# A SwiGLU block on Trainium2: a second way to split u for the three-product form, five shared PSUM banks, split weights for ten channel blocks

## The chip, the cores and the metric

One core of a Trainium2 chip runs the whole kernel. The metric is the device time of one execution in microseconds (us): the median of 3 runs, 1662.22 us before the change (1661.70 to 1662.46). The profile is one execution of the same program, with a span of 1660.3 us. The engines are TensorE (PE; its weight loads are a row of their own, PEld), VectorE (DVE), ScalarE (ACT), GpSimd (POOL) and SyncE (SP), which issues the transfers.

## The reference

An attention block with 32 inducing points feeds a feed-forward block (SwiGLU without bias). 49,664 rows of 128 channels go through both.

```python
# attention: B, N, m, C = 4, 12416, 32, 128
h = mab(I, x)            # softmax(scale * I @ x^T) @ x, over all N rows of a batch
attn_out = mab(x, h)     # softmax(scale * x @ h^T) @ h

# feed-forward: d_model 128, d_ff 1536
rms = np.sqrt(np.mean(x * x, axis=-1, keepdims=True) + 1e-06)
xn = x / rms * rms_g
g = xn @ w_gate
silu = g * (1.0 / (1.0 + np.exp(-g)))
val = xn @ w_val
return (silu * val @ w_out).astype(np.float32)
```

`u = silu * val` is the operand that the change is about: it is multiplied with `w_out` (called `wo` below) in float32 accuracy.

## The kernel before

**Units and slots.** A batch is cut into 25 units: 20 of 512 columns, 4 of 480 and 1 of 256, so there are 100 units. The 1536 channels of the feed-forward block are 12 blocks of 128 (j = 0 to 11). One unit and one block are a slot: 1200 slots. A slot has a gate matmul into one PSUM bank, silu on ScalarE, the output products that are due, a value matmul into a second bank, and the product u on VectorE.

```python
def slot(j, products, steps, tanh):
    g = ps_gv.tile([P, 512], F32, name="gv", tag="gv")
    nc.tensor.matmul(g[:, 0:T], sg[:, ts(j, P)], a[:, 0:T], start=True, stop=True)        # L657
    ...
        nc.scalar.activation(sl[:, 0:T], g[:, 0:T], AF.Silu)                              # L665
    products()
    v = ps_gv.tile([P, 512], F32, name="gv", tag="gv")
    nc.tensor.matmul(v[:, 0:T], sv[:, ts(j, P)], a[:, 0:T], start=True, stop=True)        # L668
    t = up.tile([P, 512], F32, name="u")
    ...
        nc.vector.tensor_tensor(out=t[:, 0:T], in0=sl[:, 0:T], in1=v[:, 0:T], op=ALU.mult) # L674
    steps()
    if (b, u, j) in ready:
        soon(1, lambda: three(j, t))
    else:
        plain.append(lambda: project(wo[:, j, :], t[:, 0:T]))
```

**Two forms of the output product.** In the plain form, `wo[:, j, :]` times u is one float32 matmul; the profile has it as two MATMUL and two LDWEIGHTS records. In the three-product form, u and wo are each split into a high and a low half in the type fp32r, and three fp32r matmuls take the place of the float32 one: high by high and low by low into a bank of their own (`u3`), and the product of differences into `acc`.

```python
def three(j, t):
    ...                                                     # one of 4 places in each of the rings hi, lo, d
    nc.scalar.activation(hi, v, AF.Copy, scale=1.0 - 2.0 ** -13)                          # L644
    nc.gpsimd.tensor_tensor(out=lo, in0=v, in1=hi.bitcast(F32), op=ALU.subtract)          # L645
    def rest():
        hs = third.tile([P, 512], F32, name="hs")
        nc.scalar.activation(hs[:, 0:T], hi.bitcast(F32), AF.Copy, scale=1.0 + 2.0 ** -12) # L649
        nc.gpsimd.tensor_tensor(out=d, in0=hs[:, 0:T], in1=v, op=ALU.subtract)            # L650
        kara.append((ready[b, u, j], lambda: project3(j, hi, lo, d)))
    soon(1, rest)

def project3(j, hi, lo, d):
    ...
    nc.tensor.matmul(ups[:, 0:T], w[:, i, :], hi, ...)      # L622
    nc.tensor.matmul(ups[:, 0:T], w[:, NK + i, :], lo, ...) # L624
    if not st["k"]:
        o = st["o"] = outp.tile([P, 512], F32, name="o")
        nc.scalar.activation(o[:, 0:T], ups[:, 0:T], AF.Copy, scale=1.0 + 2.0 ** -12)     # L627
    project(w[:, 2 * NK + i, :], d)                         # L606, as is the plain form
```

`soon(1, f)` runs f among the steps of the next slot. Engines take their instructions in the order in which the program has them. `finish` adds `u3` and `acc` (L614) and turns the result (L615), both on VectorE.

**Which slots take the three-product form.** The split weights exist for five blocks (`KJ` is 0, 2, 5, 7 and 9). A ledger of one server, with a slot of 1.25 us and 2.75 us for each split, chooses among these; it also gives the slot from which the three matmuls may be issued.

```python
SLOT, SPLIT, RESERVE = 1.25, 2.75, 3
...
    free = max(free, now) + busy.get(k, 0) + seam_busy.get((b, u, j), 0)
    begin = max(free, now + 2.2 * SLOT)
    if (j not in KJ or b == 0 and u < 2 or (b, u) == flat[-1] or begin > now + 3.2 * SLOT or
            any(k - 2 <= e <= k + 6 for e in marks)):
        continue
    free = begin + SPLIT
    ready[b, u, j] = int((free + 0.3) / SLOT) + 1
```

**When products are issued.** Each slot issues one product, or two if more than `RESERVE` are waiting; a three-product that has reached its slot goes first, and a plain one is kept back by at least one slot.

**PSUM.** Eight banks: four for gates and values (`ps_gv`), two for `acc`, one for `u3`, one (`ps_m`) for the attention of the next batch and the seams (the rms factors and attention weights of the next units).

Of the kernel before, what the change touches and what calls it, by code (L numbers as in the profile page):

```python
# [24 lines left out]
def kernel(  # L25
# [74 lines left out]
    KJ = [j for j in range(NJ - 2) if j % 5 in (0, 2)] + [NJ - 3]  # L100
    NK = len(KJ)
    SLOT, SPLIT, RESERVE = 1.25, 2.75, 3
# [10 lines left out]
    wp = pool("wp", NC)  # L113
# [8 lines left out]
    ps_gv = pool("ps_gv", 4, space=PSUM)  # L122
    ps_acc = pool("ps_acc", 2, space=PSUM)
    ps_u = pool("ps_u", 1, space=PSUM)
    ps_m = pool("ps_m", 1, space=PSUM)
# [30 lines left out]
    gam = const.tile([P, 1], F32, name="gam")  # L156
    nc.scalar.dma_start(out=gam[:], in_=moe_rms_g.rearrange("(c o) -> c o", o=1))
# [6 lines left out]
    bias = const.tile([P, 1], F32, name="bias")  # L164
    nc.vector.memset(bias[:], -896.0 * (1 << 23))
    ones = const.tile([P, 1], F32, name="ones")
    nc.vector.memset(ones[:], 1.0)
# [10 lines left out]
    sel = const.tile([P, 2, R, m], F32R, name="sel")  # L178
    nc.gpsimd.memset(sel[:].bitcast(F32), 0.0)
# [10 lines left out]
    ps = ps_m.tile([P, 512], F32, name="mm", tag="mm")  # L190
# [27 lines left out]
    def rounding(i, c):  # L218
# [10 lines left out]
        def numbers(name, add, mul, engine):  # L229

            t, to = st[name], st[name] if name == "e" else st[name].bitcast(F32)
            if engine is nc.scalar and name == "e":
                nc.scalar.activation(to[:], t[:], AF.Relu, bias=bias[:], scale=mul)
            elif engine is nc.scalar:
                nc.scalar.activation(to[:], t[:], AF.Copy, bias=add, scale=mul)
            else:
                engine.tensor_scalar(out=to[:], in0=t[:], scalar1=mul, scalar2=add, op0=ALU.mult, op1=ALU.add)

        def power():
            if i < 2:  # L240
                t = w0[i, c] = (silp.tile([P, 512], F32, name="silu") if (i, c) == (1, 0) else
                                 third.tile([P, 512], F32, name="hs") if (i, c) == (1, 1) else
                                 wp.tile([P, 512], F32, name="w"))
                dst = st["dst"] = t[:]
            else:
                dst = st["dst"] = wo.rearrange("p j c -> p (j c)")[:, ts(c, 512)]
            if not wide:
                nc.sync.dma_start(out=dst if i < 2 else dst.rearrange("p (j c) -> p j c", c=C), in_=source(i, c))
                return
            words = raw[i, c].rearrange("p (f w) -> p f w", w=2)  # L250
            st["low"], st["high"] = words[:, :, 0], words[:, :, 1]
            e = st["e"] = work.tile([P, 512], I32, name="we", tag="work")
            nc.vector.tensor_scalar(out=e[:], in0=st["high"], scalar1=20, scalar2=0x7FF,
                                    op0=ALU.logical_shift_right, op1=ALU.bitwise_and)
# [35 lines left out]
    lent = []  # L290

    def attention(b, load_next):
# [8 lines left out]

        def bank():
            if flowing:
                assert not lent
                return ps_m.tile([P, 512], F32, name="mm", tag="mm")
            return ps_gv.tile([P, 512], F32, name="gv", tag="gv")
# [42 lines left out]
        def max3():  # L349
            ps = bank()  # L350
            nc.tensor.matmul(ps[:, 0:1], st["row4"][:].rearrange("p q m -> p (q m)"), ones[0:1, 0:1],
                             start=True, stop=True)
            nbias = st["nbias"] = small.tile([P, 1], F32, name="nbias")
            nc.vector.tensor_copy(out=nbias[:], in_=ps[:, 0:1])
# [57 lines left out]
        def scale_h():  # L412
            hg = st["hg"] = once.tile([P, P], F32, name="hg")
            nc.vector.tensor_scalar_mul(out=hg[:], in0=st["hT"][:], scalar1=gam[:])
# [35 lines left out]
        def fetch(i):  # L450
            st["w", i] = [wp.tile([P, 512], F32, name="w") for c in range(NC)]
            for w, d in zip(st["w", i], w32[i]):
                nc.sync.dma_start(out=w[:], in_=d[:])

        def stack(i):
# [3 lines left out]
            for c, w in enumerate(st.pop(("w", i))):  # L459
                nc.tensor.matmul(ps[ts(c, m), :], st["hg"][:, 0:m], w[:], start=True, stop=True)  # L460
# [10 lines left out]
        def stack_of(i, c):  # L471

            ps = st["stack", i, c] = bank()
            nc.tensor.matmul(ps[:], st["hg"][:], w0.pop((i, c))[:], start=True, stop=True)  # L474
            nc.scalar.copy(out=stacks[b][i][:, ts(c, 512)], in_=ps[:])
# [14 lines left out]
    def seam(b, s):  # L490
# [13 lines left out]
        def square():  # L504
            assert not lent
            lent.append(s)
            ps = st["ps"] = ps_m.tile([P, 512], F32, name="mm", tag="mm")
            nc.tensor.matmul(ps[rows, 0:w], gram[b][rows, rows], st["eT"][rows, 0:w], start=True, stop=True)  # L508

        def turn_z():  # L510
            ps = st["ps"]
            lent.clear()
# [41 lines left out]
    def spread(b, u):  # L554
# [5 lines left out]
        ps = ps_gv.tile([P, 512], F32, name="gv", tag="gv")  # L560
# [7 lines left out]
    kws = {}  # L568
# [5 lines left out]
    def split_wo(step):  # L574

        if not step:
            kws["w"] = xnp.tile([P, 3 * NK, C], F32R, name=f"xn{full - 1}")
        w = kws["w"]
        whi, wlo, ws = (w[:, ts(k, NK), :] for k in range(3))
        if step == 0:  # L580
            for i, j in enumerate(KJ):
                nc.vector.tensor_scalar_mul(out=whi[:, i, :], in0=wo[:, j, :], scalar1=1.0 - 2.0 ** -13)
        if step == 1:
            for i, j in enumerate(KJ):
                nc.vector.tensor_tensor(out=wlo[:, i, :], in0=wo[:, j, :], in1=whi[:, i, :].bitcast(F32), op=ALU.subtract)
        if step == 2:
            nc.vector.tensor_scalar_mul(out=wlo, in0=wlo.bitcast(F32), scalar1=4096.0)
        if step == 3:
            nc.vector.tensor_tensor(out=ws, in0=wlo.bitcast(F32), in1=whi.bitcast(F32), op=ALU.subtract)
            for k, name in enumerate(("hi", "lo", "d")):  # L590
                kws[name] = xnp.tile([P, 4, 512], F32R, name=f"xn{full - 4 + k}")

    def ffn(b, u):
# [17 lines left out]
        def finish():  # L611
# [3 lines left out]
            nc.vector.transpose(out=o[:, 0:T], in_=(o if nk else acc)[:, 0:T])  # L615
            soon(2, lambda: store(o))

        def project3(j, hi, lo, d):
            if st["k"] == nk:
                st["u"] = ps_u.tile([P, 512], F32, name="u3")  # L620
            ups, i, w = st["u"], KJ.index(j), kws["w"]
            nc.tensor.matmul(ups[:, 0:T], w[:, i, :], hi, start=st["k"] == nk, stop=False)  # L622
            st["k"] -= 1
            nc.tensor.matmul(ups[:, 0:T], w[:, NK + i, :], lo, start=False, stop=not st["k"])  # L624
# [3 lines left out]
            project(w[:, 2 * NK + i, :], d)  # L628
# [10 lines left out]
        def three(j, t):  # L639

            n = kws["n"] = (kws.get("n", 0) + 1) % 4
            hi, lo, d = (kws[name][:, n, 0:T] for name in ("hi", "lo", "d"))
            v = t[:, 0:T]
            nc.scalar.activation(hi, v, AF.Copy, scale=1.0 - 2.0 ** -13)  # L644
            nc.gpsimd.tensor_tensor(out=lo, in0=v, in1=hi.bitcast(F32), op=ALU.subtract)  # L645

            def rest():
                hs = third.tile([P, 512], F32, name="hs")
                nc.scalar.activation(hs[:, 0:T], hi.bitcast(F32), AF.Copy, scale=1.0 + 2.0 ** -12)  # L649
                nc.gpsimd.tensor_tensor(out=d, in0=hs[:, 0:T], in1=v, op=ALU.subtract)  # L650
                kara.append((ready[b, u, j], lambda: project3(j, hi, lo, d)))

            soon(1, rest)

        def slot(j, products, steps, tanh):
            g = ps_gv.tile([P, 512], F32, name="gv", tag="gv")
# [10 lines left out]
            v = ps_gv.tile([P, 512], F32, name="gv", tag="gv")  # L667
            nc.tensor.matmul(v[:, 0:T], sv[:, ts(j, P)], a[:, 0:T], start=True, stop=True)  # L668
            t = up.tile([P, 512], F32, name="u")
# [85 lines left out]
    nc.scalar.activation(tiny[:], ones[:], AF.Silu)  # L755
# [25 lines left out]

    def schedule(b):


        plan, marks, busy = {}, [], {}

        def add(k, step, *args):
            plan.setdefault(int(k), []).append(lambda: step(*args))
            if getattr(step, "__name__", "") == "sub_max" and args[0]:
                busy[int(k)] = 1.1  # L790

        def exponentials(k, step, first):

            groups = list(range(first, NS - 1, 2))
            for i, s in enumerate(groups):
                add(k + i, step, s, NS if s == groups[-1] else s + 2)
                if i:
                    by_tanh.add((b, k + i))
            return k

        if not b:
# [8 lines left out]
            for step in range(4):  # L810
                add(18 + 2 * step, split_wo, step)
# [34 lines left out]
        return plan, marks, busy  # L846


    seams, seam_busy = {}, {}
    order = [(b, s) for b in range(B) for s in range(NS)]  # L850
    firsts = {s: min(u for u, one in enumerate(units) if one[0] == s) for s in range(NS)}
    for k, (b, s) in enumerate(order):
# [5 lines left out]
        for late_by, one in enumerate(following):  # L858
            for i, step in enumerate(seam(*one)):
# [4 lines left out]
                seam_busy[at] = seam_busy.get(at, 0) + {3: 3.0, 4: 1.2, 6: 1.4}.get(i, 0)  # L864
# [7 lines left out]
    free, ready = 0.0, {}  # L872
    for b, u in flat:
        plan, marks, busy = plans[b]
        for j in range(NJ):
            k = u * NJ + j
            now = (b * NU * NJ + k) * SLOT
            free = max(free, now) + busy.get(k, 0) + seam_busy.get((b, u, j), 0)
            begin = max(free, now + 2.2 * SLOT)
            if (j not in KJ or b == 0 and u < 2 or (b, u) == flat[-1] or begin > now + 3.2 * SLOT or  # L880
                    any(k - 2 <= e <= k + 6 for e in marks)):
                continue
            free = begin + SPLIT
            ready[b, u, j] = int((free + 0.3) / SLOT) + 1

    for b in range(B):
        plan, marks, _ = plans[b]
# [74 lines left out]
```

## Time and profile before

| | |
|---|---|
| time, median of 3 runs | 1662.22 us |
| span of the profiled execution | 1660.3 us |
| busy: PE, PEld | 1647.4 us (99%), 1037.4 us (62%) |
| busy: DVE, ACT, POOL | 1173.5, 1235.9, 1159.4 us (71, 74, 70%) |
| slots in the three-product form | 400 of 1200 (L645: 400 records) |
| granted TensorE clock | 1.000 of full speed |

The busy time of PE is the union of its records, whose ends are modelled and which overlap; how closely matmuls follow one another is read from the starts in the timeline. A group of instructions (line, engine, operation, out<-in, shape) comes with its busy time, the mean duration of one in ns, and the idle time of its engine just ahead of it with what ended it.

### The profile page before, as it was taken

How to read it: one execution, taken by the hardware profiler on the slowest of the kernel's cores; microseconds unless marked ns; L12 is line 12 of the kernel's file. 1: busy time of each engine (PE TensorE's matmuls, PEld its weight loads, DVE VectorE, ACT ScalarE, POOL GpSimd, SP SyncE). 2: the span in 40 equal slices, each digit the busy share in tenths (PEclk: the TensorE clock that was granted, in tenths of full speed). 3: DMA queues.
4: the chain of work that ended last, by engine and by line, in shares of the span. 5: the costliest groups of instructions: out<-in, count | busy, mean ns of one | idle time of the engine just before them, and what ended most of it. 6: DMA issues, size and time to landing. Idle time of an engine off the chain costs nothing.

```text
span 1660.3 us, 23265 instructions
## 1 busy us (share of the span) xinstructions
PE 1647.4 (99%) x6780; PEld 1037.4 (62%) x6780; DVE 1173.5 (71%) x1949; ACT 1235.9 (74%) x2234; POOL 1159.4 (70%) x931
## 2 busy tenths in 40 slices
PE   8999999999999999999999999999999999999998
PEld 6546566655666665665666656665567666666666
DVE  4887776676767877667677787667766666666665
ACT  4567777767787787776778777777687788788786
POOL 1347766767577775776578777577657888888885
PEclk9999999999999999999999999999999999999999
DMA  6455524333353141633335313252211111111111
GB/s 256 89 80 92 91 48 95 89 89 66 60 91 60 35 87 32 132 77 79 60 66 81 59 36 85 62 119 74 47 31 37 34 33 39 32 33 39 32 38 25
DMA packets 389167, 112.39 MB, mean 68 GB/s; under 512 B 365072, under 2 KB 369712, under 8 KB 386480
## 3 DMA queue, kind: packets, MB, share of 16 engines
q1 hardware_dynamic: 388304, 110.82, 33.0%
q8 instruction: 54, 0.88, 0.2%
q14 instruction: 73, 0.60, 0.1%
q10 hardware_dynamic: 736, 0.08, 0.0%
HBM read 53.95 MB, written 27.00 MB: 49 GB/s over the span
## 4 chain that ended last, share of the span: by engine, by line
PE 97%; DVE 2%; ACT 0%; POOL 0%; issue 0%; DVEq 0%; POOLq 0%
PE acc L606 45%; PE gv L657 17%; PE gv L668 16%; PE u L624 5%; PE u L622 5%; PE mm L330 3%; PE mm L508 1%; PE mm L386 1%; PE gv L321 0%; PE acc L187 0%; DVE u L674 0%; PE gv L330 0%; PE mm L460 0%; PE mm L474 0%; POOL rs L523 0%
## 5 line engine op out<-in xcount | busy, mean ns | idle before, releaser
L674 DVE TENSOR_TENSOR u<-silu,gv 128x512 f32<-128x512 f32 (+2 forms) x1186 | 779.8, 664 | 433.8 <-PE gv L668 228.5
L665 ACT ACTIVATE silu<-gv 128x512 f32<-128x512 f32 (+2 forms) x1186 | 691.4, 584 | 352.6 <-PE gv L657 310.0
L606 PE MATMUL acc<-u,wo 128*128 128x512 f32 (+2 forms) x1600 | 791.4, 579 | 1.2 <-DVE u L674 1.2
L668 PE MATMUL gv<-a,sv 128*128 128x512 f32 (+2 forms) x1188 | 757.7, 638 | 0.9 <-DVE u L674 0.9
L645 POOL TENSOR_TENSOR xn<-u,xn 128x512 fp32r<-128x512 f32 (+2 forms) x400 | 504.2, 1260 | 356.1 <-ACT xn L644 312.5
L650 POOL TENSOR_TENSOR xn<-hs,u 128x512 fp32r<-128x512 f32 (+2 forms) x400 | 503.9, 1260 | 32.6 <-ACT hs L649 27.8
L657 PE MATMUL gv<-a,sg 128*128 128x512 f32 (+2 forms) x1188 | 482.6, 406 | 0.0
L657 PEld LDWEIGHTS gv<-a,sg 128*128 128x128 f32 x1188 | 224.1, 189 | 228.0 <-ACT silu L665 110.8
L606 PEld LDWEIGHTS acc<-u,wo 128*128 128x128 f32 x1600 | 298.5, 188 | 79.3 <-issue 16.0
L668 PEld LDWEIGHTS gv<-a,sv 128*128 128x128 f32 x1188 | 224.0, 189 | 194.4 <-issue 133.8
L644 ACT ACTIVATE xn<-u 128x512 fp32r<-128x512 f32 (+2 forms) x400 | 247.7, 619 | 25.6 <-DVE u L674 23.4
L649 ACT ACTIVATE hs<-xn 128x512 f32<-128x512 f32 (+2 forms) x400 | 245.9, 615 | 5.6 <-POOL xn L650 4.7
L606 PE MATMUL acc<-xn,xn 128*128 128x512 f32 (+2 forms) x400 | 156.6, 391 | 0.0
L624 PE MATMUL u<-xn,xn 128*128 128x512 f32 (+2 forms) x400 | 155.6, 389 | 0.0
L622 PE MATMUL u<-xn,xn 128*128 128x512 f32 (+2 forms) x400 | 155.2, 388 | 0.0
L523 POOL TENSOR_TENSOR rs<-ms,mhalf 128x16 f32<-128x16 f32 (+2 forms) x28 | 75.9, 2711 | 16.1 <-DVE ms L521 14.0
L606 PEld LDWEIGHTS acc<-xn,xn 128*128 128x128 f32 x400 | 74.9, 187 | 19.4 <-POOL xn L650 2.8
L624 PEld LDWEIGHTS u<-xn,xn 128*128 128x128 f32 x400 | 75.1, 188 | 18.4
L622 PEld LDWEIGHTS u<-xn,xn 128*128 128x128 f32 x400 | 75.0, 188 | 16.9 <-issue 0.7
L615 DVE STREAM_TRANSPOSE o<-o 128x512 f32<-128x512 f32 (+2 forms) x97 | 67.7, 698 | 3.4
L614 DVE TENSOR_TENSOR o<-acc,o 128x512 f32<-128x512 f32 (+2 forms) x97 | 64.9, 669 | 0.1
L627 ACT ACTIVATE o<-u 128x512 f32<-128x512 f32 (+2 forms) x97 | 56.4, 581 | 0.0
(169 smaller groups left out, 769.6 us busy)
## 6 DMA issues: line engine op xcount, KB each, us to landing
out_dram<-o SPq DMA_DIRECT2D x320, 64.0 KB, 1.9
xT<-in_x_dram SPq DMA_DIRECT2D x60, 256.0 KB, 5.3
xn<-in_x_dram SPq DMA_DIRECT2D x60, 256.0 KB, 5.1
a<-hi SPq DMA_DIRECT2D x156, 64.0 KB, 2.0
a<-lo SPq DMA_DIRECT2D x156, 64.0 KB, 2.0
w<-w SPq DMA_DIRECT2D x22, 256.0 KB, 3.1
xn<-in_x_dram SPq DMA_DIRECT2D x5, 1024.0 KB, 10.3
out_dram<-o SPq DMA_DIRECT2D x64, 60.0 KB, 1.9
```

The source lines that it names most:

```text
L523: nc.gpsimd.tensor_tensor(out=rs, in0=ms, in1=mhalf[rows, 0:n], op=ALU.pow)
L606: nc.tensor.matmul(acc[:, 0:T], lhsT, rhs, start=st["left"] == NJ, stop=st["left"] == 1)
L622: nc.tensor.matmul(ups[:, 0:T], w[:, i, :], hi, start=st["k"] == nk, stop=False)
L624: nc.tensor.matmul(ups[:, 0:T], w[:, NK + i, :], lo, start=False, stop=not st["k"])
L644: nc.scalar.activation(hi, v, AF.Copy, scale=1.0 - 2.0 ** -13)
L645: nc.gpsimd.tensor_tensor(out=lo, in0=v, in1=hi.bitcast(F32), op=ALU.subtract)
L649: nc.scalar.activation(hs[:, 0:T], hi.bitcast(F32), AF.Copy, scale=1.0 + 2.0 ** -12)
L650: nc.gpsimd.tensor_tensor(out=d, in0=hs[:, 0:T], in1=v, op=ALU.subtract)
L657: nc.tensor.matmul(g[:, 0:T], sg[:, ts(j, P)], a[:, 0:T], start=True, stop=True)
L665: nc.scalar.activation(sl[:, 0:T], g[:, 0:T], AF.Silu)
L668: nc.tensor.matmul(v[:, 0:T], sv[:, ts(j, P)], a[:, 0:T], start=True, stop=True)
L674: nc.vector.tensor_tensor(out=t[:, 0:T], in0=sl[:, 0:T], in1=v[:, 0:T], op=ALU.mult)
```

## The change

The change raises how many slots can use the three-product form. It has five parts.

1. **Split weights for ten blocks** instead of five (`NK = NJ - 2`), made by ScalarE and GpSimd in eight steps, where VectorE made the five before.
2. **A second way to split u ("sums").** u stays in the PSUM bank of the value (`t = v`). ScalarE reads it once and makes the high half, already scaled by 2^-12; VectorE makes the low half; GpSimd makes the difference of the two. The way of before stays as "differences", with the roles of its two ScalarE copies rearranged.
3. **Five banks in one pool**, shared by gates, values, attention and seams, in place of four and one.
4. **A ledger per engine.** It holds, for each slot, what PE, VectorE, ScalarE and GpSimd have to do, and takes "sums", else "differences", where the backlog over the next eight slots stays within 1.2 us (VectorE, ScalarE) and 3.8 us (GpSimd).
5. Small moves: `finish` turns its result one slot after the addition; weights and constants move to other buffers to make room.

```diff
-    KJ = [j for j in range(NJ - 2) if j % 5 in (0, 2)] + [NJ - 3]
-    NK = len(KJ)
-    SLOT, SPLIT, RESERVE = 1.25, 2.75, 3
+    NK = NJ - 2
+    RING, RESERVE = 4, 3
...
-    ps_gv = pool("ps_gv", 4, space=PSUM)
+    ps_gv = pool("ps_gv", 5, space=PSUM)
     ps_acc = pool("ps_acc", 2, space=PSUM)
     ps_u = pool("ps_u", 1, space=PSUM)
-    ps_m = pool("ps_m", 1, space=PSUM)
...
-            nc.vector.transpose(out=o[:, 0:T], in_=(o if nk else acc)[:, 0:T])
-            soon(2, lambda: store(o))
+
+            def turn():
+                nc.vector.transpose(out=o[:, 0:T], in_=(o if nk else acc)[:, 0:T])
+                soon(2, lambda: store(o))
+
+            soon(1, turn)
...
-            v = t[:, 0:T]
-            nc.scalar.activation(hi, v, AF.Copy, scale=1.0 - 2.0 ** -13)
-            nc.gpsimd.tensor_tensor(out=lo, in0=v, in1=hi.bitcast(F32), op=ALU.subtract)
+            v, kind = t[:, 0:T], kinds[b, u, j]
+            if kind == "sums":
+                nc.scalar.activation(hi, v, AF.Copy, scale=(1.0 - 2.0 ** -13) * 2.0 ** -12)
+                nc.vector.scalar_tensor_tensor(out=lo, in0=hi.bitcast(F32), scalar=-4096.0, in1=v,
+                                               op0=ALU.mult, op1=ALU.add)
+            else:
+                up_ = third.tile([P, 512], F32R, name="hs")[:, 0:T]
+                nc.scalar.activation(up_, v, AF.Copy, scale=1.0 - 2.0 ** -13)
+                nc.gpsimd.tensor_tensor(out=lo, in0=v, in1=up_.bitcast(F32), op=ALU.subtract)
 
             def rest():
-                hs = third.tile([P, 512], F32, name="hs")
-                nc.scalar.activation(hs[:, 0:T], hi.bitcast(F32), AF.Copy, scale=1.0 + 2.0 ** -12)
-                nc.gpsimd.tensor_tensor(out=d, in0=hs[:, 0:T], in1=v, op=ALU.subtract)
+                if kind != "sums":
+                    nc.scalar.activation(hi, up_.bitcast(F32), AF.Copy, scale=2.0 ** -12)
+                nc.gpsimd.tensor_tensor(out=d, in0=hi.bitcast(F32), in1=lo.bitcast(F32), op=ALU.subtract)
                 kara.append((ready[b, u, j], lambda: project3(j, hi, lo, d)))
 
-            soon(1, rest)
+            if kind == "sums":
+                rest()
+            else:
+                soon(1, rest)
...
-            t = up.tile([P, 512], F32, name="u")
+            t = v if kinds.get((b, u, j)) == "sums" else up.tile([P, 512], F32, name="u")
...
+    COST = {"turn_x": (0, .65), "scores1": (1.1, .7), ... "finish": ((0, .7, .6), (0, .7)),
+            "sums": ((-.16,), (0, .7, .62, 1.27)), "differences": ((-.16,), (0, 0, .63, 1.27), (0, 0, .63, 1.27))}
+    loads = [[1.3, .68, .6, 0.0] for k in range(B * NU * NJ + 16)]
...
+    LIMIT = (0, 1.2, 1.2, 3.8)
...
+        if all(x <= max(most, y + 0.1) for now, old in zip(ahead(), before) for x, y, most in zip(now, old, LIMIT)):
+            return True
+        load(k, kind, -1)
...
+            if not (j >= NK or b == 0 and (u < 2 or n < 26) or (b, u) == flat[-1] and j > 6 or len(out_at) >= RING or
+                    any(n - 1 <= e <= n + 3 for e in marks)):
+                for kind in ("sums", "differences"):
+                    if fits(k, kind):
+                        kinds[b, u, j] = kind
+                        left, at, last = behind[3], k, k + len(COST[kind]) - 1
+                        while at <= last or left > 0:
+                            left = max(0.0, left + (loads[at][3] if at <= last else 0) - loads[at][0])
+                            at += 1
+                        ready[b, u, j] = max(at, last + 2) + 1
+                        out_at.append(ready[b, u, j] - 1)
+                        break
```

The four numbers of a cost are us on PE, VectorE, ScalarE and GpSimd; an inner tuple is one slot.

## The prediction

> **What bounds the kernel now.** I read the page first: the engine totals, then the chain that ended last.
>
> ```profile
> PE 1647.4 (99%) x6780; PEld 1037.4 (62%) x6780; DVE 1173.5 (71%) x1949; ACT 1235.9 (74%) x2234; POOL 1159.4 (70%) x931
> ...
> PE 97%; DVE 2%; ACT 0%; POOL 0%; issue 0%; DVEq 0%; POOLq 0%
> PE acc L606 45%; PE gv L657 17%; PE gv L668 16%; PE u L624 5%; PE u L622 5%; PE mm L330 3%; PE mm L508 1%; PE mm L386 1%; PE gv L321 0%; PE acc L187 0%; DVE u L674 0%; PE gv L330 0%; PE mm L460 0%; PE mm L474 0%; POOL rs L523 0%
> ```
>
> PE is busy throughout and is 97% of the chain; L606, mostly the plain float32 product, is 45% by itself. The other three engines have a quarter of the span free. So only matmul time counts, as long as nothing makes PE wait. What a matmul occupies is read from successive starts in PE's timeline (columns: start us, duration us), because its durations overlap:
>
> ```profile
> 801.60 0.39 PE L657 MATMUL gv<-a,sg 128*128 128x512 f32 x1
> 801.83 0.39 PE L622 MATMUL u<-xn,xn 128*128 128x512 f32 x1
> 802.06 0.39 PE L624 MATMUL u<-xn,xn 128*128 128x512 f32 x1
> 802.29 0.40 PE L606 MATMUL acc<-xn,xn 128*128 128x512 f32 x1
> 802.52 0.39 PE L668 MATMUL gv<-a,sv 128*128 128x512 f32 x1
> 802.75 0.39 PE L657 MATMUL gv<-a,sg 128*128 128x512 f32 x1
> 802.99 1.02 PE L606 MATMUL acc<-u,wo 128*128 128x512 f32 x2
> 803.44 0.80 PE L668 MATMUL gv<-a,sv 128*128 128x512 f32 x1
> 804.08 0.39 PE L657 MATMUL gv<-a,sg 128*128 128x480 f32 x1
> ```
>
> From gate to gate, a slot with a three-product takes 802.75 - 801.60 = 1.15 us, five fp32r matmuls at 0.23 us; one with a plain product takes 804.08 - 802.75 = 1.33 us. **A converted slot of 512 columns is worth 0.175 us** (I take 0.175, not 0.18, since other plain slots in the timeline have 1.32). With 480 columns the same reading gives 1.245 - 1.08 = 0.165 us.
>
> Then the groups by form, for what the split costs the other engines:
>
> ```profile
> L674 DVE TENSOR_TENSOR u<-silu,gv 128x512 f32<-128x512 f32 x952 | 641.6, 680 | 349.0 <-PE gv L668 173.7 <-ACT hs L649 76.1 <-ACT xn L644 65.3
> ...
> L645 POOL TENSOR_TENSOR xn<-u,xn 128x512 fp32r<-128x512 f32 x331 | 427.2, 1291 | 277.6 <-ACT xn L644 242.3 <-PE gv L657 32.7 <-PE u L622 0.3
> L650 POOL TENSOR_TENSOR xn<-hs,u 128x512 fp32r<-128x512 f32 x331 | 427.1, 1290 | 29.7 <-ACT hs L649 25.1 <-DMA w<-w 1.6
> ...
> L644 ACT ACTIVATE xn<-u 128x512 fp32r<-128x512 f32 x331 | 208.9, 631 | 22.1 <-DVE u L674 20.8
> L649 ACT ACTIVATE hs<-xn 128x512 f32<-128x512 f32 x331 | 207.3, 626 | 5.1 <-POOL xn L650 4.7
> ```
>
> A split occupies GpSimd for 2 x 1.29 = 2.58 us and ScalarE for 1.26 us. GpSimd is the dearer by far, so it is what limits the number of splits.
>
> [...] a MATMUL record lasts 0.39 us and the next starts after 0.23 us; so I count starts. [...] No trace here has VectorE writing a full tile to PSUM; I take 680 ns for that too.
>
> **Part 1, how many slots convert.** The ledger is arithmetic on numbers that the diff gives, so it can be worked through. As a check I did the old one the same way: 400 slots, 331 of 512 columns, 54 of 480, 15 of 256, just what the groups show. The new one gives **609: 406 "sums" and 203 "differences"** (491 of 512 columns, 89 of 480, 29 of 256). Of the other 591, 330 are refused for load, 200 are blocks 10 and 11, 29 lie at the exponentials, 25 at start and end, 7 for the ring. So ten blocks of weights don't double the count: it rises by 209.
>
> Gain on PE: (491 - 331) x 0.175 = 28.0; (89 - 54) x 0.165 = 5.8; 14 slots of 256 columns at about half of it, 0.08 = 1.1. Sum **35 us**. Nothing else is taken from PE. Floor: 1662.2 - 35 = **1627 us**, 2.1% less.
>
> **Part 2, the other engines.** VectorE gets 406 x 0.68 = +276 us and loses its part of the weight split, about 5: 1173 + 271 = 1444 us, 88% of some 1640. ScalarE: before 400 x 1.24 = 496; after 406 x 0.62 + 203 x 1.24 = 503, plus some 5 for weights: 1248 us, 76%. GpSimd: 1159 - 1008 + 406 x 1.29 + 203 x 2.58 = 1199 us, plus about 6 for weights, 73%. So **the load moves to VectorE**, from 71 to 88%; none passes PE in sum.
>
> **Part 3, does a split arrive in time?** If a three-product is issued before its operands are there, PE stands still, since it works in order. Before, the ledger gave it slot k+5 or k+6. Now it gives 345 of 406 "sums" slot k+4 and "differences" k+5 mostly. Timing of a "sums", from the start of its value matmul: u starts after 0.53 us (802.52 to 803.05 on VectorE) and is done at 1.22. The steps run in slot k+1, so the low half stands behind the next slot's u on VectorE, which starts at 1.25 + 0.53 and ends near 2.4; low half to 3.05; GpSimd 3.1 to 4.4. Due: in slot k+4, gate at 3 x 1.25 + 0.23, the third product at 4.68. Slack 0.3 us; with four split slots in a row, 3 x 1.15 + 0.93 = 4.38, none. Anything else on VectorE comes on top. VectorE's own pace back to back:
>
> ```profile
> 1405.50 0.69 DVE L674 TENSOR_TENSOR u<-silu,gv 128x512 f32<-128x512 f32 x1 [0.50 <-PE gv L668]
> 1406.11 0.68 DVE L614 TENSOR_TENSOR o<-acc,o 128x512 f32<-128x512 f32 x1
> 1406.82 0.71 DVE L615 STREAM_TRANSPOSE o<-o 128x512 f32<-128x512 f32 x1
> 1407.46 1.25 DVE L674 TENSOR_TENSOR u<-silu,gv 128x512 f32<-128x512 f32 x2
> ```
>
> Starts are 0.61 to 0.71 apart, 0.64 in the mean. A "sums" slot is 1.28 us of VectorE in 1.15 us of PE: a run of three leaves only 0.4 us of backlog. But `finish` (1.35 us) falls into such runs, and the seams add six instructions of 0.62 to 0.71 us (L502, L515, L516, L520, L521, L531: 4.1 us) in every fourth unit. The ledger's own backlog of VectorE in the slot after a "sums" is 0.68 us in the mean and over 0.8 us in 158 of 406, with costs of 0.68 to 0.70 where the pace is 0.64, so somewhat less in truth. I estimate that PE waits about once in each of the 95 units with splits, 0.15 to 0.2 us net (a wait lets VectorE catch up, so they don't add up): **some 15 us given back**. 1627 + 15 = **1642 us**.
>
> **The rivals.** *Full gain*: the ledger's caution suffices and PE stays as gapless as now: 1627. For it: costs in the ledger are a little above the measured pace. Against: k+4 in place of k+5. *VectorE becomes the bound*: each unit loses 0.5 us or more behind `finish`, 95 x 0.5 = 48: 1675 us. For it: 88% busy, in order, and the groups show 76 + 65 us of its idle time put down to ScalarE already. Against: its wait for PE (174 us in the row above) is the largest. *A wait for banks*: a "sums" holds its bank until 3.05 us in place of 1.22. If banks went round strictly, the gate of slot k+3, due at 2.73, would get it: 0.3 us x 406 = 120 us, to 1750. Against: the pool hands out the bank that has been free longest, so it comes round later, at the value of slot k+3 or after (3.75 us). I give this one in twenty. *The startup* (some 55 us until the first full slots) is hardly touched.
>
> **Range and chances.** Floor 1627; up to 12 us of the present time are not in my sum of pitches and might go either way; waits of 0 to 40 us. Range 1625 to 1668. Over 2% faster needs 1629 or less, nearly the floor: 0.14. Over 2% slower needs 1695, 70 us of waits: 0.08. Within 2%: 0.78.
>
> **What would show it.** L674 as often as before (x1186), 406 of them into `gv`; the low half on VectorE x406, about 680 ns; GpSimd's two subtractions x203 and x609; PE's plain L606 down to some 1182 records. A slot still 1.15 or 1.33 us. VectorE near 88%, GpSimd near 73%. If I am right on the waits, PE or PEld has idle time ahead of the difference product (L606 on split operands), ended by GpSimd or VectorE, some 15 us in all. Wrong would be: idle time ahead of gates or values ended by the low half or by ScalarE's reading of u (banks); a u written to PSUM taking clearly longer than 680 ns; or a count other than 609.

## The result and the profile after

The change made the kernel slower: 1740.7 us (median; 1740.1 to 1742.0) against 1662.1 us, a ratio of 1.047 with a 95% interval of 1.046 to 1.049. The engine totals of the changed kernel and the first line of its chain:

```profile
PE 1672.9 (96%) x6989; PEld 1046.4 (60%) x6989; DVE 1372.9 (79%) x2341; ACT 1233.3 (71%) x2250; POOL 1180.5 (68%) x947
...
PE 2%; DVE 0%; POOL 0%; ACT 0%; issue 0%; POOLq 0%; DVEq 0%; ACTq 0%
```

PE has 209 records more (two fewer for each converted plain product, three more for the three-product) and idles for 66 us where it idled for 13. The chain breaks off after 2% of the span, so it can't be read here; the waits have to be found otherwise. The groups by form, for the split's own instructions:

```profile
L674 POOL TENSOR_TENSOR xn<-xn,xn 128x512 fp32r<-128x512 f32 x491 | 628.6, 1292 | 290.8 <-DVE xn L664 147.2 <-PE gv L684 65.6 <-ACT hs L668 22.9
...
L701 DVE TENSOR_TENSOR u<-silu,gv 128x512 f32<-128x512 f32 x636 | 431.0, 679 | 144.4 <-PE gv L695 91.6 <-ACT silu L692 23.2 <-ACT xn L673 20.2
...
L701 DVE TENSOR_TENSOR gv<-silu,gv 128x512 f32<-128x512 f32 x316 | 218.5, 692 | 103.7 <-PE gv L695 66.3 <-ACT silu L692 14.5 <-ACT xn L663 12.1
...
L664 DVE SCALAR_TENSOR_TENSOR xn<-xn,gv 128x512 fp32r<-128x512 f32 x316 | 213.5, 676 | 2.1 <-ACT xn L663 1.3
L663 ACT ACTIVATE xn<-gv 128x512 fp32r<-128x512 f32 x316 | 189.8, 601 | 23.8 <-DVE gv L701 20.6
```

L674 is the difference that GpSimd makes for every split, 491 of them with 512 columns; L664, the low half on VectorE, is there 316 times with 512 columns and 406 times in all. These are the ledger's numbers. u written to PSUM takes 692 ns, u written to SBUF 679. So the counts and the durations came as predicted, and yet the time did not: the loss is in waits.

**Where the waits are.** PE's timeline in the last batch (start us, duration us):

```profile
1528.79 0.39 PE L684 MATMUL gv<-a,sg 128*128 128x512 f32 x1
1529.02 0.39 PE L636 MATMUL u<-xn,xn 128*128 128x512 f32 x1
1529.25 0.40 PE L638 MATMUL u<-xn,more 128*128 128x512 f32 x1
1529.48 0.49 PE L616 MATMUL acc<-xn,more 128*128 128x512 f32 x1
1529.81 0.40 PE L695 MATMUL gv<-a,sv 128*128 128x512 f32 x1
1530.04 0.40 PE L684 MATMUL gv<-a,sg 128*128 128x512 f32 x1
1530.28 1.02 PE L616 MATMUL acc<-u,wo 128*128 128x512 f32 x2
1530.73 0.80 PE L695 MATMUL gv<-a,sv 128*128 128x512 f32 x1
1531.37 0.40 PE L684 MATMUL gv<-a,sg 128*128 128x512 f32 x1
1531.60 0.39 PE L636 MATMUL u<-xn,xn 128*128 128x512 f32 x1
1531.84 0.40 PE L638 MATMUL u<-xn,more 128*128 128x512 f32 x1
1532.44 0.50 PE L616 MATMUL acc<-xn,more 128*128 128x512 f32 x1 [0.20 <-POOL xn L674]
1532.78 0.40 PE L695 MATMUL gv<-a,sv 128*128 128x512 f32 x1
```

The slots themselves are as before: 1530.04 to 1531.37 is a plain one, 1.33 us. But the product of differences at 1532.44 was due at 1531.84 + 0.23 = 1532.07. It came 0.37 us late, and the bracket counts only 0.20 of that as idle, because the record ahead of it is drawn to its modelled end. The first three-product costs something too: after the matmul of 1529.48 the next one starts 0.33 and not 0.23 us later. Its weight load had waited for GpSimd and started only with it:

```profile
1529.47 0.19 PEld L616 LDWEIGHTS acc<-xn,more 128*128 128x128 f32 x1 [0.26 <-POOL xn L674]
```

Over the run, 202 products of differences with 512 columns have a weight load that starts within 0.1 us of them, and the next matmul follows after 0.335 us (median); in 211 the load starts over 0.15 us ahead, and the next matmul follows after 0.233 us.

To add this up I took, for every matmul of a slot, the distance from the start ahead, less the usual distance for the same pair in the same surroundings (the tenth percentile). From 60 us on this gives 11 us for the kernel before and 120 us after: **109 us of waits**. Such sums are estimates: another choice of surroundings gives 104 us, and those below can be off by some 5 us as well. On top of the floor of 1627 us that the prediction worked out, this is 1736 us of the 1741 measured. By place: 87 us at the product of differences and right after it (before: 1.5), 10 us at the first of the three matmuls (before: 0.3), 23 us elsewhere, mostly gates, values and plain products (before: 9).

VectorE and GpSimd in the same stretch, one fence each:

```profile
1527.77 0.70 DVE L701 TENSOR_TENSOR gv<-silu,gv 128x512 f32<-128x512 f32 x1
1528.37 0.68 DVE L624 TENSOR_TENSOR o<-acc,o 128x512 f32<-128x512 f32 x1
1529.06 0.69 DVE L701 TENSOR_TENSOR gv<-silu,gv 128x512 f32<-128x512 f32 x1
1529.66 0.71 DVE L627 STREAM_TRANSPOSE o<-o 128x512 f32<-128x512 f32 x1
1530.29 0.65 DVE L664 SCALAR_TENSOR_TENSOR xn<-xn,gv 128x512 fp32r<-128x512 f32 x1
```

```profile
1531.09 2.54 POOL L674 TENSOR_TENSOR xn<-xn,xn 128x512 fp32r<-128x512 f32 x2 [1.67 <-DVE xn L664]
```

The u of 1527.77 has its low half made at 1530.29 only, behind the next u and both parts of `finish` (L624, L627), though ScalarE was done with the high half at 1529.16 (L663, 1528.56 + 0.60). GpSimd, idle for 1.67 us, starts at 1531.09 and is done near 1532.36, 4.6 us after u began. The product was due 4.3 us after u began. This is no single case: 300 weight loads of this product waited for GpSimd (total us, times, longest):

```profile
PEld acc L616 <- POOL xn L674: 131.0, 300, 1.4
```

### The profile page after: what moved, and what is told of

It reads as the page before. It is cut to its first block, busy times and chain, and to the rows that moved or that the text cites. A ratio compares the mean times of both kernels' runs of the same rounds, so it can differ in the third digit from the quotient of the medians.

```text
span 1738.5 us, 24761 instructions
## 1 busy us (share of the span) xinstructions
PE 1672.9 (96%) x6989; PEld 1046.4 (60%) x6989; DVE 1372.9 (79%) x2341; ACT 1233.3 (71%) x2250; POOL 1180.5 (68%) x947
## 5 line engine op out<-in xcount | busy, mean ns | idle before, releaser
L674 POOL TENSOR_TENSOR xn<-xn,xn 128x512 fp32r<-128x512 f32 (+2 forms) x609 | 757.3, 1255 | 337.7 <-DVE xn L664 170.8
L701 DVE TENSOR_TENSOR u<-silu,gv 128x512 f32<-128x512 f32 (+2 forms) x780 | 517.8, 666 | 183.0 <-PE gv L695 120.8
L616 PE MATMUL acc<-u,wo 128*128 128x512 f32 (+2 forms) x1182 | 587.6, 581 | 4.4 <-DVE u L701 4.3
L701 DVE TENSOR_TENSOR gv<-silu,gv 128x512 f32<-128x512 f32 (+2 forms) x406 | 272.7, 672 | 130.8 <-PE gv L695 88.7
L616 PE MATMUL acc<-xn,more 128*128 128x512 f32 (+2 forms) x609 | 263.7, 433 | 38.6 <-POOL xn L674 38.1
L669 POOL TENSOR_TENSOR xn<-u,hs 128x512 fp32r<-128x512 f32 (+2 forms) x203 | 257.1, 1266 | 29.4 <-ACT hs L668 19.1
L664 DVE SCALAR_TENSOR_TENSOR xn<-xn,gv 128x512 fp32r<-128x512 f32 (+2 forms) x406 | 266.3, 656 | 3.1 <-ACT xn L663 1.8
L663 ACT ACTIVATE xn<-gv 128x512 fp32r<-128x512 f32 (+2 forms) x406 | 237.3, 584 | 32.9 <-DVE gv L701 27.1
L668 ACT ACTIVATE hs<-u 128x512 fp32r<-128x512 f32 (+2 forms) x203 | 126.6, 624 | 77.0 <-POOL xn L669 58.9
L636 PEld LDWEIGHTS u<-xn,xn 128*128 128x128 f32 x609 | 114.5, 188 | 35.6 <-ACT o L641 12.5
L673 ACT ACTIVATE xn<-hs 128x512 fp32r<-128x512 f32 (+2 forms) x203 | 124.7, 614 | 0.0
```

The costliest lines, as they stand in the source:

```text
L616: nc.tensor.matmul(acc[:, 0:T], lhsT, rhs, start=st["left"] == NJ, stop=st["left"] == 1)
L636: nc.tensor.matmul(ups[:, 0:T], weight_of(0, j), hi, start=st["k"] == nk, stop=False)
L663: nc.scalar.activation(hi, v, AF.Copy, scale=(1.0 - 2.0 ** -13) * 2.0 ** -12)
L664: nc.vector.scalar_tensor_tensor(out=lo, in0=hi.bitcast(F32), scalar=-4096.0, in1=v, op0=ALU.mult, op1=ALU.add)
L668: nc.scalar.activation(up_, v, AF.Copy, scale=1.0 - 2.0 ** -13)
L669: nc.gpsimd.tensor_tensor(out=lo, in0=v, in1=up_.bitcast(F32), op=ALU.subtract)
```

## The experiments

Three theories. **A**: the three-product may be issued one slot too early, before GpSimd is done. **B**: u, held in its PSUM bank, keeps gates and values waiting. **C**: the second way overloads VectorE by itself.

**One slot later.** All 609 splits stay.

```diff
-                        ready[b, u, j] = max(at, last + 2) + 1
-                        out_at.append(ready[b, u, j] - 1)
+                        ready[b, u, j] = max(at, last + 2) + 2
+                        out_at.append(ready[b, u, j] - 2)
```

> All 609 splits stay as they are chosen; their three-product may be issued one slot later (about 1.25 us). Theory A, operands late: PE waits because the product of differences is issued before GpSimd has made its operand; the trace of the changed kernel has some 85 of about 110 us of PE's extra time between the second and third fp32r matmul and right after the third. One slot more gives the median chain of 4.6 us over 1 us of slack: 1640 to 1670 us. Theory B, banks: u held in a PSUM bank delays gates and values; issue time of products doesn't matter: 1735 to 1745 us.

Measured 1682.0 us, 59 us less than the changed kernel, against B, by which the issue slot wouldn't matter. It is 12 us above A's range: the waits at the product of differences fell from 87 to 9 us, but those at the first of the three matmuls grew from 10 to 21 and the others from 23 to 38. The weight loads of the product of differences show the difference in one line each (busy, mean ns, idle ahead and its end). The changed kernel:

```profile
L616 PEld LDWEIGHTS acc<-xn,more 128*128 128x128 f32 x609 | 114.0, 187 | 147.6 <-POOL xn L674 131.0
```

One slot later:

```profile
L616 PEld LDWEIGHTS acc<-xn,more 128*128 128x128 f32 x609 | 114.4, 188 | 35.1 <-POOL xn L674 12.3
```

With two slots more (below) 24 us of idle time stay ahead of these loads and none of it is put down to GpSimd, so the number to compare is what GpSimd ended: it fell from 131 to 12 us.

**u in SBUF.** The value's bank is free as soon as u is made.

```diff
-            t = v if kinds.get((b, u, j)) == "sums" else up.tile([P, 512], F32, name="u")
+            t = up.tile([P, 512], F32, name="u")
```

> u of a sums goes to an SBUF buffer as in the other form, so the bank of the value is free after the product u, as before the change; everything else is unchanged. Theory A, operands late: no change, 1730 to 1750 us. Theory B, banks: most of the 110 us come back, 1700 us or less.

Measured 1871.0 us: neither. The time alone can't refute B, as the edit brought a new cost with it. The waits can: those at gates and values, where a missing bank would show, are only some 3 us below the changed kernel's. A's number was missed by 120 us, because of something I had left out. The low half in this run, by form:

```profile
L664 DVE SCALAR_TENSOR_TENSOR xn<-xn,u 128x512 fp32r<-128x512 f32 x316 | 349.3, 1105 | 3.0 <-ACT xn L663 2.4
```

It takes 1105 ns in the mean in place of 676, with the same work. What goes with the longer ones shows when the VectorE and GpSimd rows of the trace are laid side by side:

```profile
1505.29 0.64 DVE L664 SCALAR_TENSOR_TENSOR xn<-xn,u 128x512 fp32r<-128x512 f32 x1
1505.86 0.67 DVE L701 TENSOR_TENSOR u<-silu,gv 128x512 f32<-128x512 f32 x1
1506.46 1.46 DVE L664 SCALAR_TENSOR_TENSOR xn<-xn,u 128x512 fp32r<-128x512 f32 x1
```

```profile
1503.09 1.29 POOL L674 TENSOR_TENSOR xn<-xn,xn 128x512 fp32r<-128x512 f32 x1 [0.69 <-PE acc L616]
1506.08 1.30 POOL L674 TENSOR_TENSOR xn<-xn,xn 128x512 fp32r<-128x512 f32 x1 [1.70 <-DVE xn L664]
```

The low half of 1505.29 has GpSimd idle beside it and takes 0.64 us; that of 1506.46 starts while GpSimd works until 1507.38, and takes 1.46. Over the run, 83 of 316 have no GpSimd instruction beside them (median 684 ns), 233 have (median 1384 ns). In 187 of the 233 GpSimd was already at work when the low half began, and no further GpSimd instruction began beside it (median 1452 ns); in the one case where the low half was first, it took 0.65 us and the GpSimd instruction 1.73 us. The u of 1505.86, with one input in SBUF and one in PSUM, is not slowed, and over the run 811 such instructions beside GpSimd have a median of 676 ns. In the changed kernel, with u in PSUM, 224 of the 316 low halves have a GpSimd instruction beside them and a median of 679 ns, the other 92 have 680. So keeping u in PSUM is not the fault of the change but what makes its second way affordable: with u in SBUF the same splits took 1871 us in place of 1741. The longer chain also made far more products late: waits at the product of differences went from 87 to 221 us, as A says they must.

**Differences alone.**

```diff
-                for kind in ("sums", "differences"):
+                for kind in ("differences",):
```

> The ledger may choose differences alone: worked through it gives 476 splits. Without waits PE would need 1662 - 76 x 0.17 = 1649 us. Theory A, operands late (the ledger's slot is too early for both kinds; the 203 differences of the changed kernel show about 15 us of late products): 1665 to 1690 us. Theory C, the second way alone is at fault, through its load on VectorE: 1648 to 1658 us.

Measured 1733.7 us. C falls as the only cause: without a single low half on VectorE the kernel is nearly as slow, with 476 splits. It exceeds A's range too: of 78 us of waits more than before, 22 are at the product of differences, 25 at the first of the three, 31 at gates, values and plain products. The slot can't explain all of this, as the ledger gives differences slot k+5 or later, like the old one. The waits of ScalarE and VectorE show another place to look:

```profile
DVE u L701 <- ACT silu L692: 255.0, 300, 4.0
...
ACT hs L668 <- POOL xn L669: 145.4, 179, 3.1
```

`hs` has one buffer in both kernels. Before the change it held the second ScalarE copy of a split, and ScalarE waited for GpSimd to be done with it for 4.7 us in all. Since the roles of the copies were rearranged it holds the first one, and ScalarE, which makes the silu too, waits 145 us here and 59 us in the changed kernel. VectorE's u then waits for silu, 255 us against 30 before the change. No run gave `hs` a second buffer, so how much of the loss this is stays open.

**Five blocks**, so that splits have few neighbours.

```diff
-            if not (j >= NK or b == 0 ...
+            if not (j not in (0, 2, 5, 7, 9) or b == 0 ...
```

> The new ledger and both kinds, but for the five blocks 0, 2, 5, 7 and 9 alone, so that splits have hardly a neighbour: 429 splits, 382 of them sums. Without waits 1662 - 29 x 0.17 = 1657 us. Theory A, operands late even for a lone split since the slot k+4 is too early: 1670 to 1700 us. Theory C, only runs of neighbours overload VectorE: 1655 to 1663 us.

Measured 1688.4 us, in A's range, and 31 us above its floor. Even lone splits come late: 27 us at the product of differences.

**The kernel before, one slot earlier.** The mirror image of the first run; nothing of the change is in it.

```diff
-            ready[b, u, j] = int((free + 0.3) / SLOT) + 1
+            ready[b, u, j] = int((free + 0.3) / SLOT)
```

> The kernel before the change with one thing taken from its ledger: three-products may be issued one slot earlier (k+4 in place of k+5 for most). The same 400 splits. Theory A: there the operands are done about 4.6 us after the value matmul and are due at 3 x 1.25 + 0.93 = 4.7 us, so many come late, as after the change: 1675 to 1710 us. Theory B (banks) or C (VectorE): no change, 1660 to 1665 us.

Measured 1699.7 us, a ratio of 1.023 (1.021 to 1.024) to the kernel before: 37 us lost with the same 400 splits, the same banks and no VectorE part. The waits more than before add up to 38 us, 37 of them at the product of differences. Its weight loads, first before, then one slot earlier:

```profile
L606 PEld LDWEIGHTS acc<-xn,xn 128*128 128x128 f32 x400 | 74.9, 187 | 19.4 <-POOL xn L650 2.8
```

```profile
L606 PEld LDWEIGHTS acc<-xn,xn 128*128 128x128 f32 x400 | 74.8, 187 | 68.9 <-POOL xn L650 55.6
```

This shows A by itself: one slot of lead is what kept the old kernel free of waits.

**Two slots later**, as the first run with 3 in both places.

> As the run with one slot more, but two slots more, the same 609 splits. Theory A (operands late, one slot too soon): with one slot more only 9 us were left at the product of differences, and some 48 us elsewhere (first product of a unit waiting for ScalarE to copy u3, gates and values waiting for banks); a second slot can take away at most those 9, but four places in the rings then force some products out early: 1672 to 1685 us. If lateness were still the main cause: 1650 us or less.

Measured 1663.9 us, 77 us less than the changed kernel and 8 us below the range I expected. I had counted on the product of differences alone; its waits went to 2 us, but those at the first matmul also fell, from 21 to 12.

**The u3 bank.** With one slot more, and then with two, the first three-product of a unit gives way to a plain product in the slot after ScalarE was told to copy u3:

```diff
+                turns["copied"] = turns["now"]            # where the copy of u3 is issued
...
-                    if kara and kara[0][0] <= now:
+                    fresh = kara and kara[0][2] != turns.get("unit") and now <= turns.get("copied", -9) + 1
+                    if kara and kara[0][0] <= now and not (fresh and len(plain) > 1):
```

> One slot more, and in addition the first three-product of a unit gives way to a plain product in the slot after ScalarE was told to copy u3, since the one u3 bank is not free before. If the 21 us between a gate and the first fp32r matmul are that wait: 1682 - 18 = 1664, range 1658 to 1670 us. If they are waits for the high half: no change, 1678 to 1686 us.

> Two slots more, and the first three-product of a unit gives way after the copy of u3; all 609 splits. With two slots more alone 1664 us, of which about 12 lie between a gate and the first fp32r matmul. Theory A (issue order is the cause): most of these go, 1650 to 1658 us, faster than the kernel before. If the rest are waits for banks and late silu, which move when others go: 1660 to 1666 us.

Measured 1669.9 us with one slot more (12 less than without) and 1657.9 us with two (6 less), the latter faster than the kernel before: 0.997 (0.996 to 0.998). With one slot more the waits at the first matmul fell from 21 to 6 us, so they were the u3 bank for the most part; the rest of it moved to other places.

**Tighter limits of backlog**, with one slot more and the u3 rule.

```diff
-    LIMIT = (0, 1.2, 1.2, 3.8)
+    LIMIT = (0, .8, .8, 2.5)
```

> As the run before it, with limits of backlog of 0.8 us (VectorE, ScalarE) and 2.5 us (GpSimd) in place of 1.2 and 3.8: 508 splits by the ledger's arithmetic. Without waits 1662 - 108 x 0.17 = 1644 us. If waits come from backlog on the other engines, half or more of the some 35 us that I expect with the looser limits go: 1650 to 1660 us, faster than the kernel before. If they come from the u3 bank and shared banks alone: 1660 to 1675 us.

Measured 1662.3 us, 1.000 (0.999 to 1.001), in the second range, 2 us above the first. The waits fell from 55 to 33 us, but 101 splits were given up for it, which is 17 us of matmuls. That backlog caused the waits that went isn't shown, since fewer splits also mean fewer products that can be late. (This ledger also counts a place in the rings as taken for one slot more, which leaves the count at 508.)

**Around the exponentials, and one product more in the queue.** Both on top of two slots and the u3 rule, the second on top of the first:

```diff
-                    any(n - 1 <= e <= n + 3 for e in marks)):
+                    any(n - 2 <= e <= n + 6 for e in marks)):
```

```diff
-    RING, RESERVE = 4, 3
+    RING, RESERVE = 4, 4
```

> As the run before it, and no splits in the wider stretch around the exponentials that the old kernel left free (two slots ahead to six after, in place of one and three): 599 splits, so 2 us more of matmuls. If waits of gates and values for ScalarE's late silu cluster there (about 4 us in each of the four 100 us stretches with exponentials): 1646 to 1653 us, 5 less than the run before it. If not, 2 us more than it.

> As the run before it, with one product more kept in the queue (RESERVE 4 in place of 3), so that plain products come later after their u. The plain products waited about 7 us for u with two slots more. If u is late: 5 us less than the run before it, 1642 to 1650 us. If not: the same.

Measured 1659.2 and 1652.9 us. Ten splits fewer around the exponentials cost 1.3 us and saved no waits, so that reading was wrong. A longer queue gained 6 us, about the size I expected, but not where I expected it: the waits of the plain product's weight loads for u barely moved (8.1 to 7.3 us), and gates and values waited some 7 us less. So the size was luck, and why the queue helps is open. This is the fastest version: **0.994 of the kernel before (0.993 to 0.995)**. The window from 1300 to 1600 us (columns: PE, PEld, DVE, ACT, POOL busy with counts, clock, transfers), first of the changed kernel, then of this one:

```profile
1300.00:1600.00 300.00, 292.15 (x1071) 190.33 (x1070) 243.29 (x399) 236.23 (x435) 246.07 (x194) 1.00 0.18 34
```

```profile
1300.00:1600.00 300.00, 300.00 (x1127) 210.87 (x1126) 255.61 (x414) 251.21 (x461) 268.83 (x209) 1.00 0.19 36
```

In the last batch, where no attention of a next batch runs beside, PE is gapless again, with 5% more matmuls in the same time and VectorE at 85%. What is left, 24 us more of waits than before, lies in the first three batches.

**Four banks and one**, as before the change, with two slots and the u3 rule.

```diff
-    ps_gv = pool("ps_gv", 5, space=PSUM)
+    ps_gv = pool("ps_gv", 4, space=PSUM)
+    ps_m = pool("ps_m", 1, space=PSUM)
...
+        if flowing and seam:
+            return ps_m.tile([P, 512], F32, name="mm", tag="mm")
```

> As the first of these four (two slots more, u3 rule, 609 splits), but with the banks of before: four for gates and values, one for attention and seams. Theory B in what is left (banks held by u are short): sums hold a bank for a slot longer, so gates wait more with four: 10 to 40 us more than the first of these four. If the shared pool itself makes gates wait behind the seams: 3 to 10 us less.

Measured 1708.8 us, 51 us more than with five shared banks. In its waits, the weight loads of gates (most of them behind ScalarE's silu; total us, times, longest), first with five shared banks, then with four and one:

```profile
PEld gv L686 <- ACT silu L694: 46.6, 169, 0.8
```

```profile
PEld gv L689 <- ACT silu L697: 138.8, 409, 3.3
```

So with this set of splits four banks are too few, and the five shared ones are needed: B is a cost that the change itself had for the most part met. That the longer hold of u makes four too few is likely but not shown, as no run has four banks and u in SBUF.

## Why the prediction was wrong

**Bound and gain (right).** A converted slot is worth 0.175 us, the ledger gives 609 splits, the floor is 1627 us. With two slots more and the u3 rule, all 609 splits are kept and there are some 31 us more waits than before: 1657.9 - 31 = 1627 us.

**Loads (right in size).** The low half takes 676 ns on VectorE, u in PSUM 692. VectorE's busy time is 1373 and not 1444 us. Its records add up to 250 us more than before, where I had 271 with every low half at full width; and busy time is the union of records, which overlap by some 0.08 us where they follow one another without a gap (0.69 us long, 0.61 apart), so it rose by only 199 us.

**Part 3 (the step that failed).** The prediction said: "I estimate that PE waits about once in each of the 95 units with splits, 0.15 to 0.2 us net (a wait lets VectorE catch up, so they don't add up): some 15 us given back". The mechanism was right, and so was the sign that it named, idle time ahead of the product of differences, ended by GpSimd; the term was 109 us and not 15. In place of one wait in each of 95 units there are 300. The chain's length and due time were also near: from the start of u I had 3.87 us to the finished operand and 4.15 us to when it is due; over the 406 "sums" the trace has medians of 4.07 and 4.33. What I did with these two numbers was wrong, in three ways.

1. A median slack of 0.3 us (0.15 when taken case by case) says little when the chain's length spreads from 3.65 to 5.38 us (tenth to ninetieth percentile). 193 of 406 had under 0.1 us of slack. I named the backlogs that lengthen the chain (158 of 406 over 0.8 us) and then didn't use them. The waits recur in every stretch of 100 us, at 5 to 12 us each.
2. A late operand cost PE twice: the wait itself (59 us in all) and another 0.1 us after it, where the weights weren't loaded ahead (0.335 in place of 0.233 us to the next matmul, 27 us in all). I had not counted that second cost.
3. I looked at the last of the three operands only. Waits at the first of the three, mostly for the bank of u3 (ScalarE's copy of it ended 12.5 us of idle time ahead of the first one's weight loads), and waits at gates, values and plain products cost another 24 us. The wait of ScalarE for `hs`, which the rearranged copies brought, was in no rival.

The old ledger's k+5 looked like caution that could be spent. The kernel before with one slot less shows that it was not: 37 us.

**Rivals.** The wait for banks, 1750 us, came nearest to the measured number for a wrong reason: with five banks, freeing that of u took some 3 us off the waits at gates and values; four cost 51 us. The order in which the pool hands out its banks, on which my argument against this rival rested, is not shown by any run. VectorE was not the bound, at 79% busy, though the low half stood in its queue in the stretch shown. "Full gain" holds in the last batch of the versions with two slots more and the u3 rule alone.

**Open.** The 24 us of waits left in the fastest version stand for the most part at gates, values and plain products, while the next batch's attention runs. Wider room at the exponentials didn't help, and which of the attention's steps causes them wasn't tried. Nor was a second buffer for `hs`.

## What to carry to other kernels

Where one engine is busy throughout and takes its work in order, as PE did here (99% busy before the change), the slot at which its next operand is *used* is part of the cost: compare the spread of the producing chain, not its median, with the lead, and treat lead as paid for until a run with one slot less shows that it's free. A change that puts more work on the helper engines can need more lead, not less; here the same splits took 1741 us with the ledger's slot, 1682 us one slot later and 1664 us two slots later. After such a change look at the idle time of the weight loads by operand: one row (131 us ended by GpSimd) named the largest cause.

## What the runs showed of the hardware

- u in SBUF: the low half on VectorE, with both inputs in SBUF and 512 columns, took 1384 ns (median of 233) beside GpSimd's work and 684 ns (83) without. The changed kernel, with one input in PSUM: 679 ns (224) beside GpSimd and 680 (92) without. GpSimd's own instruction (L674) rose from 1292 ns in the changed kernel to 1321 with u in SBUF, in the mean; in all but one of the 233 cases it was GpSimd that had begun first.
- The changed kernel: VectorE writing a 128x512 tile of u to PSUM, in place, took 692 ns in the mean (316), 13 ns more than to SBUF (679, 636).
- The changed kernel: a product of differences whose own weight load started only with it was followed by the next matmul after 0.335 us in place of 0.233 us (medians of 202 and 211 cases).
- The changed kernel: in the stretch shown PE and VectorE took their work in the program's order. The value matmul behind the product of differences, which GpSimd had kept until 1532.44, started at 1532.78, with its weight load at 1532.55. The low half of 1530.29, whose high half was there at 1529.16, started 1.13 us after that, behind the u of 1529.06 and L627.
